# The end of a fused attention and mixture-of-experts kernel: two instead of four dense steps held back, and the second expert layer and the output by halves of the columns

## The chip, the cores and the metric

The kernel runs on one core of one Trainium2 chip. The metric is the device time of one execution in microseconds (us); the figure for a kernel is the median of its runs.

## What is computed

Three stages follow each other: an attention with a learned relative bias, a dense two-layer network on its result, and a soft mixture of eight experts. The end of the kernel, where the change lies, is the last of them:

```python
logits = x @ phi                          # x: 2304 x 512 (the dense stage's result), phi: 512 x 32
d = softmax over the tokens of logits     # 2304 x 32
slot_input = (d.T @ x).reshape(8, 4, 512) # eight experts, four slots each
for e in range(8):
    h = np.maximum(slot_input[e] @ w1[e], 0.0)   # w1: 8 x 512 x 1024
    slot_out[e] = h @ w2[e]                      # w2: 8 x 1024 x 512
c = softmax over the slots of logits      # 2304 x 32
out = c @ slot_out.reshape(32, 512)       # 2304 x 512
```

## The kernel before

The dense stage (class `Moe`) takes the 2304 tokens in six blocks of 384 and the hidden width in 16 steps of 128, 96 steps in all. A step has an up-projection (`up`, line 686: 12 matmuls of 384 columns into `h`), a leaky activation on ScalarE and VectorE that ends in a high part and a low part of `g` (lines 694 to 706), and a down-projection (`down`, line 718: three groups of three matmuls of 512 columns, one group for each 128 tokens, into `ys`). The weights of a step are split into a high and a low part, held in one of four pairs of buffers, `h0`/`l0` to `h3`/`l3` (`wpairs`). A pair is written again four steps later. In the trace they are `w76h`, `w76l` and so on; 76 to 79 are the last four steps.

The down-projections of the last `LATE_DOWN` steps are held back until after the loop (line 966). They are then issued, in an order written out by hand in `LATE_ORDER` (lines 55 to 60), between the pieces of the routing of the last block. There ("D", i, t) is the group t of the i-th held-back step and stays in program order on TensorE. "E" copies a finished `ys` out of PSUM, "T" turns it, "L" computes the logits, "N" and "K" the softmax over the tokens, "B" turns logits and weights back, "G" sums up the slot inputs, "M" merges. The result, `rows`, is turned once more (line 1065) and copied into `sst`, the stationary operand of the first expert layer.

The expert stage (class `Experts`) reads 64 tiles of expert weights, each 128 x 1024 in fp32 (512 KB): 32 of `w1` and 32 of `w2`, in the order of `self.order` (line 1021). `load` (line 1023) puts the next tile of that order into the buffer it is handed, called a home. There are 37 homes: five in `pre` (loaded two blocks ahead), three in `ex`, 15 in `ep` (the dense stage's raw weight buffers, freed step by step), five in `er` (a ring over memory that the dense stage gives back), one in `g32` and eight in `em`, the four weight pairs. Those of `er`, `g32` and `em` are asked for when the dense stage is over, in `Experts.run` (lines 1044 to 1048). The other 27 tiles go into homes that the first expert layer has finished with (line 1088). All DMAs of this stretch are issued by SyncE, in one queue. A scheduler that models the timeline when the program is built puts each engine's instructions in order; that order is fixed on the chip.

A tile belongs to expert 4k + j, and its matmuls write the 32 rows 32j to 32j + 31 of PSUM, so that four tiles with different j can use four column groups of TensorE beside each other. The first layer writes `hps` (two banks of 512 columns), the second `ops` (one bank of 512 columns). An fp32 matmul call shows as two instructions in the trace, so a tile is four instructions in either layer. Between the layers `hps` goes through the ReLU and is turned into `gst` (line 1096). After the second layer `ops` is copied and corrected into `st` (lines 1106 and 1107), multiplied by the token weights `cT` for 18 groups of 128 tokens (line 1114), copied out of PSUM by ScalarE and VectorE in turn (lines 1116 and 1118), and written by nine DMAs of 512 KB (line 1119) from homes that are free.

Of the kernel before, what the change touches and what calls it, by code (L numbers as in the profile page):

```python
# [8 lines left out]
F32 = mybir.dt.float32  # L9
F32R = mybir.dt.float32r  # L10
# [3 lines left out]
AF = mybir.ActivationFunctionType  # L14
ALU = mybir.AluOpType
AX = mybir.AxisListType
PSUM = bass.MemoryType.PSUM
DRAM = bass.MemoryType.DRAM

P = 128  # L20
B, H, S, D = 4, 8, 576, 64
HP = H // 2
N = B * S
DM = H * D
DFF = 2048
NF = DFF // P
NC = DM // P
SLOTS = 32
E = 8
SPE = SLOTS // E  # L30
F2 = 1024
NT = 384
NBLK = N // NT
# [15 lines left out]
ERING = 5  # L49
# [1 line left out]
XF = 10  # L51
LAG = 2
WL_DVE = ((0, 3), (0, 4), (0, 5), (0, 6), (0, 7), (0, 8), (0, 11), (0, 13), (0, 14), (1, 2), (1, 3), (1, 4), (1, 5), (1, 6), (1, 9), (1, 10), (1, 12), (1, 13), (2, 0), (2, 1), (2, 3), (2, 9), (2, 12), (2, 13), (2, 15), (3, 4), (3, 9), (3, 11), (3, 13), (3, 15), (4, 5), (4, 8), (4, 9), (4, 12), (4, 13), (4, 14), (5, 3), (5, 4), (5, 5), (5, 7), (5, 8), (5, 9), (5, 12))
LATE_DOWN = 4
LATE_ORDER = (
# [4 lines left out]
)  # L60
GL_POOL = (0,)
# [481 lines left out]
class Moe:  # L543
# [134 lines left out]
    def up(self, n):  # L678
        nc = self.nc
        blk, f = self.seq[n]  # L680
        xh, xl = self.x[blk]
        wh, wl = self.ws[blk if blk > 1 else 0, f]
        h = self.ps_h.tile([P, NT], F32, tag="h", name=f"h{n}")
        for c in range(NC):
            for n_, (w_, x_) in enumerate(((wh, xh), (wh, xl), (wl, xh))):
                nc.tensor.matmul(  # L686
                    h,
                    w_[:, c * P : (c + 1) * P],
                    x_[:, c],
                    start=c == 0 and n_ == 0,  # L690
                    stop=c == NC - 1 and n_ == 2,
                )
        g = self.g32[:, NT * (n % 2) : NT * (n % 2) + NT]
        nc.scalar.activation(g, h, AF.Relu)  # L694
        neg = self.g32[:, 2 * NT : 3 * NT]
        nc.scalar.activation(neg, h, AF.Relu, scale=-1.0)  # L696
        nc.vector.scalar_tensor_tensor(g, neg, self.nal[:, f : f + 1], g, ALU.mult, ALU.add)  # L697
        hold = n == NBLK * NF - LATE_DOWN
        if hold:
            gh, gl = (p.tile([P, NT], F32R, tag=tag, name=f"{tag}_{n}") for p, tag in self.raws)  # L700
        else:
            gh, gl = (self.gr[:, NT * k : NT * k + NT] for k in (self.ng % 3, 3 + self.ng % 3))
            self.ng += 1
        nc.scalar.activation(gh, g, AF.Copy)  # L704
        eng = nc.gpsimd if blk in GL_POOL else nc.vector
        eng.tensor_tensor(gl, g, gh.bitcast(F32), ALU.subtract)  # L706
        return gh, gl
# [301 lines left out]
class Experts:  # L1009
# [3 lines left out]
    def __init__(self, nc, w1, w2):  # L1013
        self.nc = nc
        self.tiles = []
        self.homes = []
        self.free = []
        w1 = w1.rearrange("e (p c) n -> e p c n", c=NC)
        w2 = w2.rearrange("e (p a b) n -> e p a (b n)", a=4, b=2)

        self.order = [(w, k, a, j) for w in (w1, w2) for k in range(2) for a in range(4) for j in range(4)]

    def load(self, home):

# [10 lines left out]
    def run(self, tc, moe, scon, out, more):  # L1035
        nc = self.nc
        cT, sst = moe.cT, self.sst.rearrange("p (e c m) -> p e c m", e=E, c=NC)
        with ExitStack() as ctx:
            er = ctx.enter_context(tc.tile_pool(name="e_ring", bufs=1, reuse_waits="tile"))
            ep = ctx.enter_context(tc.tile_pool(name="e_sb", bufs=1, reuse_waits="tile"))  # L1040
            ps_a = ctx.enter_context(tc.tile_pool(name="e_ps_a", bufs=1, space=PSUM, reuse_waits="tile"))
            ps_b = ctx.enter_context(tc.tile_pool(name="e_ps_b", bufs=5, space=PSUM, reuse_waits="tile"))

            for n in range(ERING):
                self.load(lambda k, n=n: er.tile([P, 1024], F32, tag=f"er{n}", name=f"er{k}"))
            self.load(lambda k: moe.g32[:, :1024])
            for pool, tag in more:
                self.load(lambda k, pool=pool, tag=tag: pool.tile([P, 1024], F32, tag=tag, name=f"em{k}"))
            sc = ep.tile([P, P + 1], F32, name="sc")
            nc.sync.dma_start(sc, scon)  # L1050
            gst = ep.tile([P, E, 8, SLOTS], F32, name="gst")
# [19 lines left out]
                do["S"](ep, "cs", ps_b)  # L1071

            hps = ps_a.tile([P, 2, 512], F32, name="hps")
            ops = ps_a.tile([P, 512], F32, name="ops")
            hs = ep.tile([P, 1024], F32, name="hs")
            for n, (w, k, a, j) in enumerate(self.order):
                t = self.tiles[n]
                rows = slice(32 * j, 32 * j + 32)
                first, last = k == 0 and a == 0, k == 1 and a == 3
                for b in range(2):  # L1080
                    if n < 32:
                        dst, lhs = hps[rows, b], sst[:, 4 * k + j, a]
                        f, l = first, last
                    else:
                        dst, lhs = ops[rows], gst[:, 4 * k + j, 2 * a + b]
                        f, l = first and b == 0, last and b == 1
                    nc.tensor.matmul(dst, lhs, t[:, 512 * b : 512 * b + 512], start=f, stop=l)  # L1087
                self.load(self.homes[n])
                if n == 31:
                    nc.scalar.activation(hs[:, :512], hps[:, 0], AF.Relu)  # L1090
                    nc.vector.tensor_scalar(hs[:, 512:], hps[:, 1], 0.0, None, ALU.max)
                    for h in range(2):
                        tp = ps_b.tile([P, 4, P], F32, tag="b", name=f"turn1_{h}")
                        for c in range(4):
                            lhs = hs.rearrange("r (p c) -> r c p", c=8)[:, 4 * h + c]
                            nc.tensor.matmul(tp[:, c], lhs, sc[:, :P], start=True, stop=True)  # L1096
                        for g in range(2):
                            src = tp.rearrange("p c (j k m) -> p k j c m", k=2, m=16)[:, g]
                            fill(g, gst[:, 4 * g : 4 * g + 4, 4 * h : 4 * h + 4, 16 * g : 16 * g + 16], src)


            hi = ep.tile([P, 512], F32R, name="hi")
            st = ep.tile([P, 512], F32R, name="st")
            for h in range(2):
                c = slice(256 * h, 256 * h + 256)
                nc.scalar.activation(hi[:, c], ops[:, c], AF.Copy)
                nc.vector.scalar_tensor_tensor(
                    st[:, c], hi[:, c].bitcast(F32), sc[:, P:], ops[:, c], ALU.mult, ALU.add
                )
            for t in range(0, N // P, 2):  # L1110
                os_ = self.free.pop(0)(f"o{t}").rearrange("p (a n) -> p a n", a=2)
                for a in range(2):
                    o = ps_b.tile([P, 512], F32, tag="b", name=f"o{t}_{a}")
                    nc.tensor.matmul(o, cT[:, (t + a) * P : (t + a + 1) * P], st, start=True, stop=True)
                    if a:
                        nc.vector.tensor_copy(os_[:, a], o)
                    else:
                        nc.scalar.activation(os_[:, a], o, AF.Copy)
                nc.sync.dma_start(out[t * P : (t + 2) * P].rearrange("(a p) n -> p a n", p=P), os_)


@with_exitstack
def kernel(
    ctx, tc, qk, v_l, cpack, w_l, alpha, phi, mw1, mw2, lcol, prow, xmain, xtail, scon, out
):
    nc = tc.nc
# [67 lines left out]
    def prefetch(n):  # L1194
        f = n - (NBLK - 1) * NF
        if n == 4 * NF:
            t = set0["bias"].tile([P, 9 * S], F32, tag="nb", name="pre")
            for j in range(5):
                ex.load(lambda k, j=j: t[:, 1024 * j : 1024 * j + 1024])
        elif f == XF:  # L1200
            t = x0.tile([P, 3072], F32, tag="x", name="ex")
            for j in range(3):
                ex.load(lambda k, j=j: t[:, 1024 * j : 1024 * j + 1024])

        if f == -2:
            ex.sst = moe.raw_tile(0, "sst")
            nc.gpsimd.memset(ex.sst, 0.0)
        if 1 <= f + 3 < NF:
            ex.load(lambda k: moe.raw_tile(f + 3, f"ep{k}"))

    with ExitStack() as mctx:
        moe.run(mctx, phi, prefetch)
    more = [(kp, t) for t in ("h0", "l0", "h1", "l1")] + [(ws, t) for t in ("h2", "l2", "h3", "l3")]
    ex.run(tc, moe, scon, out, more)


# [31 lines left out]
def _layout(i):  # L1248
# [29 lines left out]
        alpha=i["moe_alpha"].reshape(NF, P).T,  # L1278
        phi=i["moe2_phi"].reshape(NC, P, 2, 4, SPE).transpose(1, 0, 3, 2, 4).reshape(P, NC, SLOTS),
        mw1=i["moe2_w1"],  # L1280
        mw2=i["moe2_w2"],
    )


# [27 lines left out]
```

## Time and profile before

| | us |
|---|---|
| median of 3 runs | 828.95 |
| lowest and highest | 828.21 and 831.59 |
| the profiled execution | 829.09 |
| span of the profiled execution, first to last instruction | 827.3 |

The profile is of one execution. Its engines are PE (TensorE matmul), PEld (TensorE weight load, which overlaps PE), DVE (VectorE), ACT (ScalarE), POOL (GpSimd) and SP (SyncE; SPq is its queue). Times in a row are us from the start of the span unless marked ns, and L1087 is line 1087 of the kernel before. `out<-in` names what an instruction writes and reads, x32 is a count, and what stands in brackets is the idle time before the first of the row and what ended it. PEclk is the granted TensorE clock as a share of full speed.

### The profile page before, as it was taken

The numbers are of one execution on the slowest core, as the hardware profiler recorded it, in microseconds if no ns is written. First come the engines' busy times: TensorE is split into PE (matmuls) and PEld (weight loads), VectorE is DVE, ScalarE is ACT, GpSimd is POOL, SyncE is SP. The second block draws the span as 40 slices with busy tenths as digits, with TensorE's granted clock in tenths as the row PEclk, the third lists the DMA queues.
The fourth block names the chain that finished last, engine by engine and source line by source line (L and its number), as shares of the span: only waits on it lengthen the run. The fifth ranks groups of instructions, "written<-read, shape, count | busy, mean of one in ns | idle before, by whom it ended". The sixth has DMA issues, their size and how long they took to land.

```text
span 827.3 us, 18364 instructions
## 1 busy us (share of the span) xinstructions
PE 769.7 (93%) x7428; PEld 639.3 (77%) x7428; DVE 552.8 (67%) x951; ACT 487.3 (59%) x961; POOL 339.6 (41%) x259
## 2 busy tenths in 40 slices
PE   6876699999999999999999999999999999998993
PEld 6766577778777768988888988888889898885431
DVE  8956668888898857776778565655675756565003
ACT  8852477888888874444356566656566656554002
POOL 6974324546467532113224454445444551231000
PEclk9989789999999999999999999999999999999998
DMA  6799894956844351342240011301100134338996
GB/s 211 184 220 204 196 251 147 235 168 187 239 137 146 95 176 70 114 153 101 103 128 1 1 29 42 134 1 39 39 1 21 29 114 141 90 115 298 383 363 229
DMA packets 59493, 114.44 MB, mean 138 GB/s; under 512 B 10640, under 2 KB 38160, under 8 KB 57360
## 3 DMA queue, kind: packets, MB, share of 16 engines
q1 hardware_dynamic: 59408, 113.26, 45.2%
q8 instruction: 58, 0.95, 0.5%
q14 instruction: 27, 0.22, 0.1%
HBM read 91.95 MB, written 21.29 MB: 137 GB/s over the span
## 4 chain that ended last, share of the span: by engine, by line
PE 82%; DVE 7%; issue 4%; ACT 2%; DMA 2%; POOL 2%; DVEq 0%; ACTq 0%; SPq 0%; POOLq 0%
PE h L686 23%; PE ys L718 22%; PE o L467 10%; PE s L381 8%; PE acc L161 5%; PE t L439 5%; PE ops L1087 3%; PE hps L1087 2%; DVE mask L145 1%; DVE z L399 1%; PE lp L778 1%; DMA W<-rows 1%; DVE r L485 1%; PE turn L1096 0%; DVE x L605 0%
## 5 line engine op out<-in xcount | busy, mean ns | idle before, releaser
L697 DVE SCALAR_TENSOR_TENSOR g<-g,nal 128x384 f32<-128x384 f32 x96 | 99.6, 1038 | 83.1 <-ACT g L696 82.9
L419 ACT ACTIVATE e<-z,m 128x576 f32<-128x576 f32 x144 | 109.9, 767 | 17.6 <-DVE m L399 17.6
L399 DVE CUSTOM_DVE_ANT_0 z<-s,nb 128x576 f32<-128x576 f32 x144 | 108.1, 755 | 17.3 <-PE s L381 10.5
L704 ACT ACTIVATE gr<-g 128x384 fp32r<-128x384 f32 x95 | 49.7, 523 | 85.7 <-DVE g L697 85.6
L467 PE MATMUL o<-g,v 128*64 128x256 f32 (+1 forms) x640 | 87.4, 419 | 0.5 <-ACT g L455 0.5
L455 ACT ACTIVATE g<-t 128x640 f32<-128x640 f32 x96 | 67.2, 703 | 34.6 <-PE t L439 30.8
L694 ACT ACTIVATE g<-h 128x384 f32<-128x384 f32 x96 | 46.8, 488 | 57.4 <-PE h L686 55.1
L161 PE MATMUL acc<-wp,mask 128*128 128x64 bf16 (+1 forms) x1680 | 58.6, 200 | 21.2 <-issue 11.9
L706 DVE TENSOR_TENSOR gr<-g,gr 128x384 fp32r<-128x384 f32 x79 | 53.5, 677 | 34.0 <-ACT gr L704 31.7
L161 PEld LDWEIGHTS <-mask 128*128 128x128 bf16 (+1 forms) x1680 | 56.6, 105 | 23.1 <-issue 14.3
L439 PE MATMUL t<-ident,e 64*128 64x64 f32 x1440 | 68.8, 224 | 5.0 <-DVE m L399 3.0
L439 PEld LDWEIGHTS t<-ident,e 64*128 64x128 f32 x1440 | 66.0, 140 | 7.3 <-issue 5.0
L381 PE MATMUL s<-kh,qh 64*128 64x288 f32 x320 | 61.9, 382 | 8.0 <-DVE rows L186 5.2
L467 PEld LDWEIGHTS o<-g,v 128*64 128x64 f32 x640 | 44.1, 139 | 29.4 <-issue 1.5
L142 ACT ACTIVATE mask<-pr,wb 128x576 bf16<-128x576 f16 (+4 forms) x81 | 47.0, 665 | 22.4 <-PE acc L161 22.4
L354 POOL TENSOR_SCALAR qh<-raw 128x1216 fp32r<-128x1216 f32 x16 | 19.4, 1214 | 79.7 <-PE s L381 75.6
L706 POOL TENSOR_TENSOR gr<-g,gr 128x384 fp32r<-128x384 f32 x16 | 19.6, 1228 | 78.4 <-ACT gr L704 68.6
L381 PE MATMUL s<-kl,qh 64*128 64x288 f32 x320 | 48.6, 299 | 0.0
L381 PE MATMUL s<-kh,ql 64*128 64x288 f32 x320 | 48.5, 298 | 0.0
L696 ACT ACTIVATE g<-h 128x384 f32<-128x384 f32 x96 | 46.6, 485 | 0.0
L381 PEld LDWEIGHTS s<-kh,qh 64*128 64x128 f32 x320 | 31.8, 194 | 17.5 <-issue 7.2
L356 POOL TENSOR_TENSOR ql<-raw,qh 128x1216 fp32r<-128x1216 f32 x16 | 44.7, 2795 | 0.0
(986 smaller groups left out, 2045.4 us busy)
## 6 DMA issues: line engine op xcount, KB each, us to landing
wide<-in_w_dram SPq DMA_DIRECT2D x16, 1024.0 KB
ep<-in_mw_dram SPq DMA_DIRECT2D x30, 512.0 KB
raw<-in_qk_dram SPq DMA_DIRECT2D x16, 896.0 KB
nb<-W SPq DMA_DIRECT2D x12, 576.0 KB
v<-in_v_l_dram SPq DMA_DIRECT2D x16, 320.0 KB
pre<-in_mw_dram SPq DMA_DIRECT2D x10, 512.0 KB
er<-in_mw_dram SPq DMA_DIRECT2D x9, 512.0 KB
em<-in_mw_dram SPq DMA_DIRECT2D x8, 512.0 KB
```

The source lines that it names most:

```text
L161: nc.tensor.matmul(dst[:, u // 8, :, :, 4 * (u % 8) : 4 * (u % 8) + 4], mask[:, (16 * k + u) % RING, cols], wp[:, part], start=part == 0, ...
L381: nc.tensor.matmul(s[:, hf, :288], st["q", a][d, o : o + P], st["k", b][d, 288 * h : 288 * h + 288], start=n_ == 0, stop=n_ == len(seq) - 1,),
L399: self.nc.vector.tensor_tensor_reduce(out=z.rearrange("p (a b) -> p a b", a=2), in0=s[:, :, :288], in1=self.nb[st["hp"]][:, slot].rearrang ...
L419: self.nc.scalar.activation(e, z, AF.Exp, bias=m, scale=-1.0, accum_out=st["sum"][:, slot : slot + 1]),
L439: self.pin(i, nc.tensor.transpose(tp[:, r, 64 * c : 64 * c + 64], e[q, k0 : k0 + P], self.ident[q, q]))
L455: self.pin(i, nc.scalar.activation(dst, src, AF.Copy))
L467: nc.tensor.matmul(op[64 * h : 64 * h + 64, 0, :n], st["v"][:, h, c], g[:, h, c], start=c == 0, stop=c == 4),
L686: nc.tensor.matmul(h, w_[:, c * P : (c + 1) * P], x_[:, c], start=c == 0 and n_ == 0, stop=c == NC - 1 and n_ == 2,)
L697: nc.vector.scalar_tensor_tensor(g, neg, self.nal[:, f : f + 1], g, ALU.mult, ALU.add)
L704: nc.scalar.activation(gh, g, AF.Copy)
L706: eng.tensor_tensor(gl, g, gh.bitcast(F32), ALU.subtract)
L718: i = self.nc.tensor.matmul(self.ys[blk][t], g_[:, t * P : (t + 1) * P], w_[:, 512:], start=f == 0 and n_ == 0, stop=f == NF - 1 and n_ == 2,)
```

## The change

Two down-projections instead of four are held back: those of steps 76 and 77 run in the loop, and `LATE_ORDER` is shorter by their six groups. The separate buffers of the first held-back step's `g` are gone. The weight pairs of these two steps are asked for in `prefetch`, right behind their down-projections; the two other pairs, `g32` and then the ring follow after the loop, so the same 37 homes are taken in another order. `w2` is laid out on the host by halves of its columns: 16 tiles carry columns 0 to 255, 16 tiles columns 256 to 511, and a tile holds four blocks of 256 columns in place of two of 512. The second layer runs the first 16 tiles, then `finish(0)`, then the other 16, then `finish(1)`. `finish` copies and corrects that half, multiplies it by the token weights, and writes it with five DMAs (four of 512 KB, one of 256 KB), whose rows in memory are 256 columns long. `ops` takes two banks of PSUM, and the pool of the turns and outputs four instead of five.

```diff
...
 XF = 10
 LAG = 2
-LATE_DOWN = 4
+LATE_DOWN = 2
 LATE_ORDER = (
-    ("D", 0, 0), ("D", 1, 0), ("D", 2, 0), ("D", 0, 1), ("D", 1, 1), ("D", 3, 0), ("E", 0), ("D", 2, 1),
-    ("D", 3, 1), ("E", 1), ("D", 0, 2), ("T", 0), ("D", 1, 2), ("T", 1), ("D", 2, 2),
-    ("D", 3, 2), ("E", 2), ("L", 0), ("L", 1), ("N", 0), ("K", 0), ("T", 2), ("L", 2), ("N", 1),
+    ("D", 0, 0), ("D", 1, 0), ("E", 0), ("D", 0, 1), ("D", 1, 1), ("E", 1), ("T", 0), ("D", 0, 2), ("T", 1), ("D", 1, 2),
+    ("E", 2), ("L", 0), ("L", 1), ("N", 0), ("K", 0), ("T", 2), ("L", 2), ("N", 1),
     ("B", 0), ("K", 1), ("B", 1), ("G", 0), ("G", 1), ("M",),
 )
 GL_POOL = (0,)
...
         neg = self.g32[:, 2 * NT : 3 * NT]
         nc.scalar.activation(neg, h, AF.Relu, scale=-1.0)
         nc.vector.scalar_tensor_tensor(g, neg, self.nal[:, f : f + 1], g, ALU.mult, ALU.add)
-        hold = n == NBLK * NF - LATE_DOWN
-        if hold:
-            gh, gl = (p.tile([P, NT], F32R, tag=tag, name=f"{tag}_{n}") for p, tag in self.raws)
-        else:
-            gh, gl = (self.gr[:, NT * k : NT * k + NT] for k in (self.ng % 3, 3 + self.ng % 3))
-            self.ng += 1
+        gh, gl = (self.gr[:, NT * k : NT * k + NT] for k in (self.ng % 3, 3 + self.ng % 3))
+        self.ng += 1
         nc.scalar.activation(gh, g, AF.Copy)
         eng = nc.gpsimd if blk in GL_POOL else nc.vector
         eng.tensor_tensor(gl, g, gh.bitcast(F32), ALU.subtract)
...
         self.homes = []
         self.free = []
         w1 = w1.rearrange("e (p c) n -> e p c n", c=NC)
-        w2 = w2.rearrange("e (p a b) n -> e p a (b n)", a=4, b=2)
-
-        self.order = [(w, k, a, j) for w in (w1, w2) for k in range(2) for a in range(4) for j in range(4)]
+        self.order = [(w1, k, a, j) for k in range(2) for a in range(4) for j in range(4)]
+        self.order += [(w2[c], k, a, j) for c in range(2) for k in range(2) for a in range(2) for j in range(4)]
 
     def load(self, home):
 
...
             er = ctx.enter_context(tc.tile_pool(name="e_ring", bufs=1, reuse_waits="tile"))
             ep = ctx.enter_context(tc.tile_pool(name="e_sb", bufs=1, reuse_waits="tile"))
             ps_a = ctx.enter_context(tc.tile_pool(name="e_ps_a", bufs=1, space=PSUM, reuse_waits="tile"))
-            ps_b = ctx.enter_context(tc.tile_pool(name="e_ps_b", bufs=5, space=PSUM, reuse_waits="tile"))
-
-            for n in range(ERING):
-                self.load(lambda k, n=n: er.tile([P, 1024], F32, tag=f"er{n}", name=f"er{k}"))
+            ps_b = ctx.enter_context(tc.tile_pool(name="e_ps_b", bufs=4, space=PSUM, reuse_waits="tile"))
+
             self.load(lambda k: moe.g32[:, :1024])
             for pool, tag in more:
                 self.load(lambda k, pool=pool, tag=tag: pool.tile([P, 1024], F32, tag=tag, name=f"em{k}"))
+            for n in range(ERING):
+                self.load(lambda k, n=n: er.tile([P, 1024], F32, tag=f"er{n}", name=f"er{k}"))
             sc = ep.tile([P, P + 1], F32, name="sc")
             nc.sync.dma_start(sc, scon)
             gst = ep.tile([P, E, 8, SLOTS], F32, name="gst")
...
                 do["S"](ep, "cs", ps_b)
 
             hps = ps_a.tile([P, 2, 512], F32, name="hps")
-            ops = ps_a.tile([P, 512], F32, name="ops")
+            ops = ps_a.tile([P, 2, 512], F32, name="ops")
             hs = ep.tile([P, 1024], F32, name="hs")
+            hi = ep.tile([P, 2, 256], F32R, name="hi")
+            st = ep.tile([P, 2, 256], F32R, name="st")
+
+            def finish(c):
+
+                nc.scalar.activation(hi[:, c], ops[:, c, :256], AF.Copy)
+                nc.vector.scalar_tensor_tensor(
+                    st[:, c], hi[:, c].bitcast(F32), sc[:, P:], ops[:, c, :256], ALU.mult, ALU.add
+                )
+                for t in range(0, N // P, 4):
+                    m = min(4, N // P - t)
+                    os_ = self.free.pop(0)(f"o{t}_{c}")[:, : 256 * m].rearrange("p (a n) -> p a n", a=m)
+                    for a in range(0, m, 2):
+                        o = ps_b.tile([P, 2, 256], F32, tag="b", name=f"o{t}_{a}_{c}")
+                        for k in range(2):
+                            q = (t + a + k) * P
+                            nc.tensor.matmul(o[:, k], cT[:, q : q + P], st[:, c], start=True, stop=True)
+                        if a:
+                            nc.vector.tensor_copy(os_[:, a : a + 2], o)
+                        else:
+                            nc.scalar.activation(os_[:, a : a + 2], o, AF.Copy)
+                    nc.sync.dma_start(
+                        out[t * P : (t + m) * P, 256 * c : 256 * c + 256].rearrange("(a p) n -> p a n", p=P), os_
+                    )
+
             for n, (w, k, a, j) in enumerate(self.order):
                 t = self.tiles[n]
                 rows = slice(32 * j, 32 * j + 32)
-                first, last = k == 0 and a == 0, k == 1 and a == 3
-                for b in range(2):
-                    if n < 32:
-                        dst, lhs = hps[rows, b], sst[:, 4 * k + j, a]
-                        f, l = first, last
-                    else:
-                        dst, lhs = ops[rows], gst[:, 4 * k + j, 2 * a + b]
-                        f, l = first and b == 0, last and b == 1
-                    nc.tensor.matmul(dst, lhs, t[:, 512 * b : 512 * b + 512], start=f, stop=l)
+                if n < 32:
+                    first, last = k == 0 and a == 0, k == 1 and a == 3
+                    for b in range(2):
+                        nc.tensor.matmul(
+                            hps[rows, b], sst[:, 4 * k + j, a], t[:, 512 * b : 512 * b + 512], start=first, stop=last
+                        )
+                else:
+                    c = (n - 32) // 16
+                    for b in range(4):
+                        nc.tensor.matmul(
+                            ops[rows, c, :256],
+                            gst[:, 4 * k + j, 4 * a + b],
+                            t[:, 256 * b : 256 * b + 256],
+                            start=k + a + b == 0,
+                            stop=(k, a, b) == (1, 1, 3),
+                        )
                 self.load(self.homes[n])
                 if n == 31:
                     nc.scalar.activation(hs[:, :512], hps[:, 0], AF.Relu)
...
                         for g in range(2):
                             src = tp.rearrange("p c (j k m) -> p k j c m", k=2, m=16)[:, g]
                             fill(g, gst[:, 4 * g : 4 * g + 4, 4 * h : 4 * h + 4, 16 * g : 16 * g + 16], src)
-
-
-            hi = ep.tile([P, 512], F32R, name="hi")
-            st = ep.tile([P, 512], F32R, name="st")
-            for h in range(2):
-                c = slice(256 * h, 256 * h + 256)
-                nc.scalar.activation(hi[:, c], ops[:, c], AF.Copy)
-                nc.vector.scalar_tensor_tensor(
-                    st[:, c], hi[:, c].bitcast(F32), sc[:, P:], ops[:, c], ALU.mult, ALU.add
-                )
-            for t in range(0, N // P, 2):
-                os_ = self.free.pop(0)(f"o{t}").rearrange("p (a n) -> p a n", a=2)
-                for a in range(2):
-                    o = ps_b.tile([P, 512], F32, tag="b", name=f"o{t}_{a}")
-                    nc.tensor.matmul(o, cT[:, (t + a) * P : (t + a + 1) * P], st, start=True, stop=True)
-                    if a:
-                        nc.vector.tensor_copy(os_[:, a], o)
-                    else:
-                        nc.scalar.activation(os_[:, a], o, AF.Copy)
-                nc.sync.dma_start(out[t * P : (t + 2) * P].rearrange("(a p) n -> p a n", p=P), os_)
+                if n in (47, 63):
+                    finish((n - 47) // 16)
 
 
 @with_exitstack
...
             nc.gpsimd.memset(ex.sst, 0.0)
         if 1 <= f + 3 < NF:
             ex.load(lambda k: moe.raw_tile(f + 3, f"ep{k}"))
+        if 0 <= f - (NF - 4) < 4 - LATE_DOWN:
+            pool, *tags = moe.wpairs[f - (NF - 4)]
+            for tag in tags:
+                ex.load(lambda k, tag=tag: pool.tile([P, 1024], F32, tag=tag, name=f"em{k}"))
 
     with ExitStack() as mctx:
         moe.run(mctx, phi, prefetch)
-    more = [(kp, t) for t in ("h0", "l0", "h1", "l1")] + [(ws, t) for t in ("h2", "l2", "h3", "l3")]
+    more = [(pool, t) for pool, *tags in moe.wpairs[4 - LATE_DOWN :] for t in tags]
     ex.run(tc, moe, scon, out, more)
 
 
...
         alpha=i["moe_alpha"].reshape(NF, P).T,
         phi=i["moe2_phi"].reshape(NC, P, 2, 4, SPE).transpose(1, 0, 3, 2, 4).reshape(P, NC, SLOTS),
         mw1=i["moe2_w1"],
-        mw2=i["moe2_w2"],
+        mw2=i["moe2_w2"].reshape(E, P, 2, 4, 2, 256).transpose(4, 0, 1, 2, 3, 5).reshape(2, E, P, 2, 1024),
     )
 
 
```

## Rows read from the trace of the kernel before

**Rows 1.** The chain of waits in order of time: start us, us, what.

```profile
742.34 6.26 PE ys L718 x27
...
763.31 5.93 PE hps L1087 x32
...
786.05 22.54 PE ops L1087 x128
```

**Rows 2.** Windows: start:end length, busy us of each engine, PEclk, DMA share, GB/s.

```profile
744.00:745.00 1.00, 1.00 (x6) 0.81 (x6) 0.61 (x1) 0.36 (x1) 0.00 (x0) 1.00 0.00 0
768.00:770.00 2.00, 2.00 (x19) 0.51 (x15) 0.32 (x2) 0.35 (x1) 0.00 (x0) 1.00 0.95 278
804.00:805.00 1.00, 1.00 (x4) 0.25 (x3) 0.00 (x0) 0.00 (x0) 0.00 (x0) 1.00 0.31 123
813.00:814.00 1.00, 1.00 (x5) 0.43 (x4) 1.00 (x3) 1.00 (x3) 0.00 (x0) 1.00 0.99 371
825.00:826.00 1.00, 0.00 (x0) 0.00 (x0) 0.00 (x0) 0.00 (x0) 0.00 (x0) 0.50 0.51 186
```

**Rows 3.** DMA packets from 776 to 803 us, while weights arrive.

```profile
DMA packets 3038, 11.08 MB, mean 410 GB/s; under 512 B 339, under 2 KB 339, under 8 KB 3036
```

**Rows 4.** DMA packets from 814 to 824 us, while the output leaves.

```profile
DMA packets 1954, 3.78 MB, mean 378 GB/s; under 512 B 112, under 2 KB 112, under 8 KB 1953
```

**Rows 5.** SyncE's queue in order of time: start us, us, what is issued.

```profile
745.79 0.33 SPq L1031 DMA_DIRECT2D g<-in_mw_dram  x1
748.40 4.92 SPq L1031 DMA_DIRECT2D em<-in_mw_dram  x8
...
766.96 2.62 SPq L1031 DMA_DIRECT2D pre<-in_mw_dram  x5
...
792.69 4.15 SPq L1031 DMA_DIRECT2D er<-in_mw_dram  x4
```

**Rows 6.** Order of time, TensorE's weight loads in the second layer, early and late.

```profile
793.30 0.20 PEld L1087 LDWEIGHTS ops<-ep,gst 128*32 128x32 f32 x4 [0.23 <-issue]
793.73 0.20 PEld L1087 LDWEIGHTS ops<-ep,gst 128*32 128x32 f32 x4 [0.23 <-issue]
...
804.18 0.14 PEld L1087 LDWEIGHTS ops<-er,gst 128*32 128x32 f32 x2 [0.29 <-DMA er<-in_mw_dram]
804.64 0.11 PEld L1087 LDWEIGHTS ops<-er,gst 128*32 128x32 f32 x1 [0.32 <-issue]
805.07 0.11 PEld L1087 LDWEIGHTS ops<-er,gst 128*32 128x32 f32 x1 [0.32 <-issue]
805.42 0.14 PEld L1087 LDWEIGHTS ops<-er,gst 128*32 128x32 f32 x2 [0.24 <-DMA er<-in_mw_dram]
```

**Rows 7.** Order of time around dense step 79: weight load, last up-projection matmul, low half.

```profile
740.31 0.19 PEld L686 LDWEIGHTS h<-x,w79l 128*128 128x128 f32 x1 [0.66 <-POOL w79l L675]
...
742.00 0.34 PE L686 MATMUL h<-x,w79l 128*128 128x384 f32 x1
...
745.20 0.56 DVE L706 TENSOR_TENSOR gr<-g,gr 128x384 fp32r<-128x384 f32 x1 [0.59 <-ACT gr L704]
```

**Rows 8.** Line 1114, the output matmuls' weight loads: ns min/median/max, first and last start.

```profile
L1114 PEld LDWEIGHTS o<-st,cT x18: 186/187/190, 810.6 to 815.2; 128*128 128x128 f32 x18
```

**Rows 9.** Order of time, TensorE, two transposes between waves of `hps`.

```profile
768.63 0.61 PE L1087 MATMUL hps<-ep,sst 128*32 128x512 f32 x3
769.17 0.44 PE L887 MATMUL tc<-ident,cs 128*128 128x128 f32 x2
769.54 3.68 PE L1087 MATMUL hps<-ep,sst 128*32 128x512 f32 x32
```

**Rows 10.** Order of time after the second layer: the copy and `st`.

```profile
808.61 0.38 ACT L1106 ACTIVATE hi<-ops 128x256 fp32r<-128x256 f32 x1 [22.14 <-PE ops L1087]
809.03 0.48 DVE L1107 SCALAR_TENSOR_TENSOR st<-hi,sc,ops 128x256 fp32r<-128x256 f32 x1 [22.10 <-ACT hi L1106]
```

**Rows 11.** DMA packets from 40 to 60 us, a stretch of small packets.

```profile
DMA packets 6310, 4.78 MB, mean 239 GB/s; under 512 B 1660, under 2 KB 6264, under 8 KB 6306
```

## The prediction, made before the changed kernel was built or run

> **What bounds the kernel now.** I read the chain that ended last in order of time, then the stretches from 738 us on in short windows, then the queue of SyncE, then TensorE's own order. The change touches nothing before 734 us. From there the chain [rows 1] is TensorE nearly without a break: dense matmuls to about 752, a routing tail through ACT and DVE, the first expert layer from 763.3, the turn of its result, and the second expert layer, 22.5 us of `ops` from 786.05 to 808.6. Then comes a tail with little on TensorE. The windows [rows 2] show the other resource. The DMA engines are idle at 744 to 745, then busy with weights until about 804.5, and busy again, with the output, from 813.0 to 825.5. Weights move at 410 GB/s in 4 KB packets [rows 3], the output at 378 GB/s in 2 KB packets [rows 4].
>
> The queue [rows 5] shows who feeds whom. SyncE issues the load into `g32` at 745.8, eight into the weight pairs from 748.4, the ring's behind them, and the first refill only at 767.0, after the first wave of `hps` has freed a buffer. The last four weights go out from 792.7.
>
> TensorE's order explains the 22.5 us. Four tiles of one round fill four column groups. Early in the layer weight loads come in fours every 0.43 us [rows 6]: four instructions per wave, a tile (four instructions) costs 0.43 us. Late, they come as two, one, one within 1.24 to 1.28 us: each tile runs by itself, since its four instructions add to the same rows of PSUM one behind the other. Of the 32 tiles the last 10 or so (from 795.2) go like that: 22 x 0.43 + 10 x 1.3 = 22.5, the row. Data ended at 804.5, TensorE at 808.6: the end of this layer is TensorE's, with the weights close behind.
>
> **Part 1: two steps held back, not four.** No work goes away. Down 76 and 77 (27 matmuls took 6.26 us [rows 1], so 0.232 each, nine per step = 2.09 us) now run in the loop, ahead of the up-projection of 79. Before, that up-projection waited 0.7 us for POOL's `w79l` [rows 7]; with the downs ahead of it that wait goes. In exchange a wait appears. The low half of 79's `g` came 3.4 us after its `h` (742.34 to 745.76 [rows 7]). Five thirds of down steps (0.70 each) covered that; now one does, D(0,0), and D(1,0) needs `g` of 79. The wait is at most 3.4 - 0.7 = 2.7 us; ScalarE is freer than it was, which takes off some 0.7, so 2.0. Queued behind it on TensorE are all pinned D steps, and behind those the turns, logits and sums. The rest of the tail (E, T, L, N, B, G) has the same instructions with less cover. Working it through by the durations above, the last D ends about 1.0 us later, and so does `hps`: 764.3. Bounds: 0 (the waits cancel) to 2.7.
>
> **Part 2: buffers taken sooner.** Four loads (2.1 MB, 5.1 us at 410 GB/s) move from 748 to about 740 to 745, where the queue was nearly empty. SyncE waits there in order for down 76, then 77; behind it stand only `g32` and the other expert loads, and none is needed before 763. I cost this at nothing, gain included. There are 37 buffers as before, and the other 27 tiles can't go out before `hps` frees one. Before, the backlog ended just as the refills began (768 to 770 is the dip, 278 GB/s [rows 2]); now it ends earlier and the engines idle until the first refill at about 768. The 27 refills end 1.0 us later than before: 805.5.
>
> **Part 3: second layer by halves.** 64 calls of 512 columns become 128 of 256: the same columns. First half: 32 waves of 0.215 = 7.0 us if waves of four keep up. The four weight loads of a wave span 0.20 us [rows 6], so it is close; at 0.25 it is 8.0. I take 7.0: 787.0 to 794.0. All its 16 tiles are there by then (tile 47 is the eleventh refill, about 784). A tile that runs alone now has a chain of eight instructions of 0.213, one overlapped with the next tile: 1.5 us, where it was 1.28.
>
> Then 18 output matmuls of 256 columns join TensorE's queue before or among the second half. Their weight loads take 187 ns each [rows 8], more than the 0.117 us that 256 columns would stream at the rate of the `ys` matmuls [rows 1]: 18 x 0.18 = 3.2 us. The far bounds are 2.1 us (streaming alone) and 4.4, which is nine interruptions at the price of the two transposes that broke into `hps`: start to start 0.91 instead of 0.42 [rows 9], 0.49 each. I take 3.2, as it rests on the same instruction.
>
> That price has a rule beside it: the Trainium skill, TensorEngine Tiling (Array Packing), Key Properties, says that changing the tiling mode drains the engine, and this change puts full-width matmuls among column-tiled ones. By that rule alone the 4.4 would hold and the forecast would rise by 1.2 us.
>
> Second half: 16 x 0.43 = 6.9 us, plus 1.07 us (1.5 - 0.43) for each tile that runs alone. How many? Before, TensorE met the arrivals with 10 tiles left at 795.2. Now it stands there at 787.0 + 7.0 + 3.2 + 6 x 0.43 = 799.8, 4.6 us later, while arrivals shift by 1.0. Of the 3.6 us in hand each tile eats 0.86 (arrivals every 1.29, four-wide 0.43): 4.2 tiles, so 5.8 are left. The layer ends at 787.0 + 7.0 + 3.2 + 6.9 + 5.8 x 1.07 = 810.3, against 808.6. Bounds: 808.4 (no tile short of the data; last landing plus one chain of eight, with no shift from part 1) and 814.8 (10 alone, as before).
>
> **Part 4: output by halves.** Before, from the layer's end: copy and `st` twice [rows 10], data moving at 813.0 (4.4 us), 12.5 us of transfer, 1.8 us to the end of the span: 18.7. Now one half's copy and `st` (0.38 + 0.48 and two gaps of 0.04) come before the first output matmul, so data move 3.6 us after the end, and half as many bytes follow. The first half's output (2.36 MB) is queued when the last weights have been issued (about 798) and moves behind them from 805.5. Its rows are now 1 KB. Per engine, 4 KB packets take 160 ns (410 / 16) and 2 KB packets 86.7 ns (378 / 16); a line through both gives 50 ns for 1 KB, which is 328 GB/s, 7.2 us per half (an estimate from [rows 3, 4]). Bounds: 6.2 us at the 2 KB rate, 9.9 at the 239 GB/s of a stretch whose packets average 757 B [rows 11]. I stay at 7.2, nearest to the output's own row.
>
> The Trainium skill, DMA: Bandwidth & Descriptors, Why small descriptors are slow, gives a fixed cost of about 3 cycles per packet beside one per 32 bytes; an estimate by that is 35 beats for 32 of data, 0.957 of the 2 KB rate, 6.5 us per half and a forecast 0.7 us lower.
>
> The first half is out by 805.5 + 7.2 = 812.7, before the second starts at 810.3 + 3.6 = 813.9, so the covered half is free. Evacuation (nine copies of 0.6 to 0.7 us on two engines) stays under the transfer.
>
> **Sum.** Span after: 810.3 + 3.6 + 7.2 + 1.8 = 822.9, against 827.3. The profiled execution took 829.09 us for that span, 1.8 more, and 0.14 over the median of 828.95. So 822.9 + 1.8 = 824.7 us. Put otherwise: about 7 us come off the tail, 1.0 goes back in the held-back steps and 0.7 more in the second layer, and 1.0 to the smaller rows is inside the 7.
>
> **Rivals.** (a) The gain in full: no shift from part 1, TensorE close to the data, output rows as fast as 2 KB ones: 808.4 + 3.6 + 6.2 + 1.8 = 820.0, so 822 us. For it: the weights did end 4 us ahead of TensorE. Against: the wait for `g` of 79 is plain. (b) As many tiles run alone as before: 814.8, span 827.4, 829.2 us, no change. For it: the order is fixed when the program is built, and that they ran alone though the data were there late in the layer shows that it does not follow the chip. (c) The first half's output gets into SyncE's queue ahead of the last weights, 7.2 us later for these, landing 812.7, layer end 816.6, 831.0 us. Against: the last weights are issued by 797.8, the first output is ready at about 796.6, so at most a few cross. (d) Slower: all 16 tiles of the second half run alone, at 1.5 us: 787.0 + 7.0 + 3.2 + 24 = 821.2, span 833.8, 835.6 us. It turns into a loss from 10 tiles alone. For it: chains are now eight long; against: most of these tiles have landed by 798. That the earlier loads themselves bring something would show as an earlier last landing; I count it in (a).
>
> **How the numbers follow.** Forecast 50%, its own range 822.5 to 827; (a) 16%, (b) 17%, (c) 6%, (d) 11%. Half a per cent (4.1 us, about what a measurement tells from no change) sets the limits at 824.8 and 833.1. The forecast lies on the first, so its chance splits, 28 to 22. Faster: 28 + 16 = 44%. Same: 22 + 17 + 5 = 44%. Slower: 11 + 1 = 12%. The range, 821 to 831, leaves out (d) and the ends of (a) and (c).
>
> **What would show it.** A wait of about 2 us of an `ys` matmul for `gr` near 746; `hps` starting near 764.3; DMA idle before 768; the last weights landing near 805.5; `ops` of the first half in some 7 us; five or six tiles at 1.5 us; output moving without a gap behind the weights, and 7 us of it after the layer's end. The prediction is wrong if `hps` starts earlier than 763, if the weight loads of the second half come singly from its first tile, or if 1 KB rows move below 280 GB/s.

## The result and the profile after

| | before | after |
|---|---|---|
| median, us | 829.84 (5 runs, 828.21 to 831.59) | 839.35 (5 runs, 834.34 to 839.75) |
| the profiled execution, us | 829.09 | 837.57 |
| its span, us | 827.3 | 835.8 |

The ratio is 1.0108, interval [1.0077, 1.0138]: slower by 1.1%, where 824.7 us and at most 831 were forecast.

The profile stays the place to see where. Stretches far ahead of the change differ by some microseconds between profiled executions (the first matmul of step 75's up-projection stands between 719.1 and 724.0 us in the eleven profiles of this study), so I count from that instruction: 723.10 before, 722.67 after.

| from, to | before, us | after, us | difference |
|---|---|---|---|
| up 75 to first `hps` | 40.21 | 41.92 | +1.71 |
| first `hps` to second layer | 22.74 | 22.63 | -0.11 |
| second layer, to its last end | 22.54 | 36.75 | +14.21 |
| its end to the end of the span | 18.71 | 11.83 | -6.88 |
| sum | 104.20 | 113.13 | +8.93 |

The chain of waits of the changed kernel in order of time (start us, us, what; it answers to [rows 1]):

```profile
747.66 2.47 PE ys L713 x9
...
764.59 5.69 PE hps L1101 x32
...
787.22 16.24 PE ops L1107 x128
803.48 0.39 ACT hi L1075
803.90 0.49 DVE st L1076
804.44 1.21 PE o L1086 x8
805.65 4.09 PE ops L1107 x30
809.74 1.15 PE o L1086 x8
810.89 2.74 PE ops L1107 x18
813.63 0.43 PE o L1086 x2
814.07 9.90 PE ops L1107 x80
...
824.94 2.91 PE o L1086 x18
```

The first half of the second layer took 16.24 us, where 7.0 was forecast. The second took 20.5: 16.7 in `ops`, 2.8 in the 18 output matmuls, and 1.0 in which TensorE stood still for the first half's `hi` and `st`.

TensorE's order of time shows how its tiles pass. Each row is a run of matmuls that read the same kind of buffer; the start is what matters here, since four instructions of one tile follow each other in steps of 0.21 us:

```profile
792.60 0.40 PE L1107 MATMUL ops<-pre,gst 128*32 128x256 f32 x1
792.81 0.38 PE L1107 MATMUL ops<-er,gst 128*32 128x256 f32 x1
792.84 0.38 PE L1107 MATMUL ops<-pre,gst 128*32 128x256 f32 x1
793.02 0.38 PE L1107 MATMUL ops<-er,gst 128*32 128x256 f32 x1
793.05 0.38 PE L1107 MATMUL ops<-pre,gst 128*32 128x256 f32 x1
793.24 0.38 PE L1107 MATMUL ops<-er,gst 128*32 128x256 f32 x1
793.27 4.17 PE L1107 MATMUL ops<-pre,gst 128*32 128x256 f32 x34
797.07 0.40 PE L1107 MATMUL ops<-ep,gst 128*32 128x256 f32 x1
...
814.00 3.05 PE L1107 MATMUL ops<-ex,gst 128*32 128x256 f32 x21
816.67 0.40 PE L1107 MATMUL ops<-ep,gst 128*32 128x256 f32 x1
```

The first `pre` tile enters beside the last four instructions of an `er` tile: two tiles run beside each other, never four. The next kind of buffer follows after five tiles (797.07 - 792.60) and after three (816.67 - 814.00): 0.89 us a tile, 4.2 steps of 0.2135. Before, a tile passed in 0.43 [rows 6]. None of these rows has a wait in brackets. The windows (start:end length, busy us of PE, PEld, DVE, ACT, POOL, then PEclk, DMA share, GB/s) show the other resource:

```profile
766.00:768.00 2.00, 2.00 (x12) 0.39 (x5) 0.39 (x3) 0.00 (x0) 0.00 (x0) 0.50 0.22 80
...
786.00:788.00 2.00, 2.00 (x7) 1.28 (x7) 0.47 (x2) 0.38 (x1) 0.00 (x0) 0.50 1.01 395
788.00:790.00 2.00, 2.00 (x13) 0.97 (x13) 0.10 (x1) 0.00 (x0) 0.00 (x0) 0.69 1.03 416
...
818.00:824.00 6.00, 5.95 (x50) 3.23 (x46) 0.00 (x0) 0.01 (x1) 0.00 (x0) 1.00 0.00 0
```

For the last 6 us of the layer nothing moves at all: all weights are there, the first half's output is gone. The queue of SyncE answers to [rows 5]:

```profile
768.24 2.40 SPq L1025 DMA_DIRECT2D pre<-in_mw_dram  x5
...
793.57 4.16 SPq L1025 DMA_DIRECT2D em<-in_mw_dram  x4
805.96 0.40 SPq L1091 DMA_DIRECT2D out_dram<-g  x1
...
826.49 4.74 SPq L1091 DMA_DIRECT2D out_dram<-ero  x5
```

The refills follow `hps` as they did, and the first half's output is issued at 806.0, not at about 798 as forecast.

### The profile page after: what moved, and what is told of

Same layout as the page of the kernel before. It is cut to its first block, busy times and chain, and to the rows that moved or that the text cites. A ratio compares the mean times of both kernels' runs of the same rounds, so it can differ in the third digit from the quotient of the medians.

```text
span 835.8 us, 18663 instructions
## 1 busy us (share of the span) xinstructions
PE 779.1 (93%) x7574; PEld 651.0 (78%) x7574; DVE 550.0 (66%) x950; ACT 488.0 (58%) x962; POOL 339.0 (41%) x259
## 4 chain that ended last, share of the span: by engine, by line
PE 83%; DVE 6%; issue 4%; DMA 2%; ACT 2%; POOL 1%; SPq 0%; DVEq 0%; ACTq 0%; POOLq 0%
PE h L685 23%; PE ys L713 21%; PE o L466 10%; PE s L380 8%; PE t L438 5%; PE acc L160 5%; PE ops L1107 4%; PE hps L1101 2%; DMA W<-rows 2%; DVE mask L144 1%; PE lp L773 1%; DVE z L398 1%; PE o L1086 1%; PE turn L1122 1%; DVE r L484 1%
```

## The experiments

**The theory** after this result: what costs the time is the length of a run, the number of instructions that a column group gets behind one another. Program order is tile by tile in both kernels: the programs as built hand TensorE the calls of this layer so, the scheduler did not mix the tiles, and what runs beside what is therefore settled on the chip. As long as a tile is four instructions, TensorE lets the next groups pass beside it; with eight, about four of them stand in the way until they have gone through. **The rivals**: the output matmuls among the tiles, the two steps that are no longer held back, narrower instructions that cost more in themselves, and the reading of the prediction, that tiles run alone where TensorE's order puts them so. Time ratios are to runs of the kernel before on the same chip; "stretch" is the time from up 75 to the end of the span, 104.20 before and 113.13 after.

**The changed kernel with the second layer in turns**, one call of each of the four tiles, then the next:

```diff
-                else:
+                elif j == 3:
...
-                    for b in range(4):
...
+                    for b0 in range(0, 4, 1):
+                        for i in range(4):
+                            for b in range(b0, b0 + 1):
+                                nc.tensor.matmul(
+                                    ops[32 * i : 32 * i + 32, c, :256],
...
```

> The changed kernel with one edit: in the second expert layer the four tiles of a round take turns call by call (block of columns outside, tile inside), so a column group gets two instructions at a visit instead of eight. Theory 1 (runs): TensorE takes its instructions in order and holds only about four for one column group, so eight behind each other for one group keep the other groups waiting; turns bring back waves of four at 0.215 us, 7 to 8 us per half instead of 16.2, the first half's output then fills the time of the last weights, layer end near 809, 821 to 824 us. Theory 2 (price of the instruction): a 256-column matmul with its weight load costs about 0.12 us whatever the order; then 836 to 839 us, as the changed kernel.

821.65 us, ratio 0.9931 [0.9909, 0.9953], stretch 98.92. Its chain, and a piece of TensorE's order:

```profile
785.99 8.07 PE ops L1109 x128
...
806.71 1.93 PE ops L1109 x26
808.66 0.39 ACT hi L1075
```

```profile
789.08 0.38 PE L1109 MATMUL ops<-er,gst 128*32 128x256 f32 x1
789.09 0.39 PE L1109 MATMUL ops<-pre,gst 128*32 128x256 f32 x3
789.30 0.38 PE L1109 MATMUL ops<-er,gst 128*32 128x256 f32 x1
789.30 0.39 PE L1109 MATMUL ops<-pre,gst 128*32 128x256 f32 x3
...
806.71 1.91 PE L1109 MATMUL ops<-em,gst 128*32 128x256 f32 x26 [0.63 <-DMA em<-in_mw_dram]
```

Four tiles start together every 0.21 us, the first half takes 8.07 us (PEclk is 0.51 from 786 to 788), and the layer ends on the landing of the last weights: the last tile waits for it until 806.71. The same matmuls, with as many output matmuls among them, take 14.2 us less in the stretch: the order alone makes the loss, and the narrow instructions in themselves do not.

**Two calls at a visit**, so runs of four instructions (the edit is against the kernel with turns):

```diff
-                    for b0 in range(0, 4, 1):
+                    for b0 in range(0, 4, 2):
...
-                            for b in range(b0, b0 + 1):
+                            for b in range(b0, b0 + 2):
```

> As the kernel with turns, but two calls (four instructions) at a visit. Theory 1 with four held for a column group: the same time as with turns call by call, within 1 us. Theory 1 with fewer than four held: a tile of four instructions still blocks, 827 to 832 us. Theory 2: 836 to 839 us.

822.32 us, 0.9945 [0.9919, 0.9971], stretch 98.67: as with one. Runs of four still pass beside each other.

**Three calls, then one** (runs of six and two; the edit is against the kernel with two calls):

```diff
-                    for b0 in range(0, 4, 2):
+                    for b0 in (0, 3):
...
-                            for b in range(b0, b0 + 2):
+                            for b in range(b0, min(b0 + 3, 4)):
```

> The changed kernel with the second layer's round visited in turns of three calls and then one, so that a column group gets six instructions behind one another and later two. If a tile of eight costs 0.895 us because about four instructions of a run can be held back while the next group's go on, the next group starts with the third of the six, and the rounds of the first half come at about 10 to 12 slots of 0.2135 us, where turns of one or two calls need 8 and whole tiles 16.8: the first half takes about 9 to 11 us (it took 8.07 with turns of one call, 16.24 as changed), and the whole stays at 822 to 825 us, since the last tiles wait for their landing. If any run that is longer than four goes two wide as a run of eight does, the first half takes about 13 us or more.

One execution; its chain:

```profile
789.37 10.08 PE ops L1109 x128
```

The first half took 10.08 us, inside the 9 to 11 of the theory and not the 13 of a sharp limit. PEclk was 1.00 there, so the times to set beside it are those at full clock further down: 7.11 us in turns and 15.26 us with runs of eight. The whole was 828.4 us, 3 above the range given: by then TensorE and not the landing ended the second half (6.88 us for its last 84 instructions).

**The kernel before with runs of eight in its first layer** (two tiles of one column group behind each other, 512 columns as ever):

```diff
+                    if a % 2 and j == 3:
+                        for i in range(4):
+                            for a_ in (a - 1, a):
...
+                                for b in range(2):
```

> The kernel before, the first expert layer alone reordered: two tiles of one column group behind each other, so eight instructions of 512 columns per visit instead of four; same matmuls, same sums. If about four are held for a group: the next group starts with the fifth of the eight, 16 visits of 4 x 0.427 = 1.71 us and a tail of 1.7, plus about 3 for the half clock at its start: hps takes 29 to 32 us instead of 17.2. If the changed kernel's slowness was that of 256 columns: hps stays 17 to 18 us.

One execution, 836.96 us. The chain:

```profile
759.35 11.70 PE hps L1086 x32
...
771.41 8.79 PE hps L1086 x32
...
780.47 15.79 PE hps L1086 x64
...
801.84 14.41 PE ops L1097 x128
```

The layer took 37 us, where it took 17.3 (763.31 [rows 1] to 780.6, the start of the ReLU), with neither the halves nor the output near it, and none of its matmul rows behind the first has a wait in brackets. That is more than was expected, in its first round above all, which ran partly at half clock (PEclk 0.50 from 759 to 765). The other two parts give the same period as the changed kernel: eight steps of 0.427 for the last run, and (15.79 - 3.42) / 7 = 1.77 us for each before it, 4.1 steps. And the second layer, untouched, then took 14.41 us, since its weights had long landed.

**Two steps held back, alone, in the kernel before** (the early loads and the order of homes with it):

```diff
-LATE_DOWN = 4
+LATE_DOWN = 2
...
+        if 0 <= f - (NF - 4) < 4 - LATE_DOWN:
+            pool, *tags = moe.wpairs[f - (NF - 4)]
```

> The kernel before with the first two parts of the change alone: two steps held back, their pairs loaded sooner, order of the homes as changed; second layer and output as before. If the wait for the activation of step 79 is the price and the earlier loads bring nothing: 1.0 to 1.5 us slower than before, 830.5 to 831.5. If the earlier loads pay: as before or up to 4 us faster, 825 to 830.

828.75 us, 1.0014 [0.9998, 1.0029], stretch 106.31, 2.1 more: by the time it can't be told from no change, and the earlier loads do not pay. TensorE's order shows the wait, and a window of 2 us shows DMA engines that have run out of homes:

```profile
744.08 0.51 PE L713 MATMUL ys<-w79h,gr 128*128 128x512 f32 x1 [1.54 <-ACT gr L699]
```

```profile
763.00:765.00 2.00, 2.00 (x16) 0.51 (x12) 0.00 (x0) 0.00 (x0) 0.00 (x0) 0.68 0.00 1
```

**The changed kernel with four held back**, tile by tile as it was:

```diff
-LATE_DOWN = 2
+LATE_DOWN = 4
```

> The changed kernel with four steps held back again (order by hand, separate buffers and pairs as before); halves of the columns stay. If holding back two costs what the trace shows (hps 1.3 us later), and the earlier loads bring nothing: 1.0 to 1.5 us faster than the changed kernel, 836 to 838. If the earlier loads are worth their 5 us of transfer: slower than the changed kernel, 841 to 844.

```profile
787.23 15.26 PE ops L1112 x128
```

833.25 us, 1.008 [1.0049, 1.0111], stretch 110.80: still slower. The stretch is 2.3 of the 8.9 shorter: 1.7 in `hps`, which starts 40.17 us after up 75 again, and 1.0 in the first half of `ops`, less 0.4 between the layers. Only the 1.7 can be put down to holding back. The 1.0 is the clock: this half ran at a PEclk of 1.00, while the changed kernel had 0.50 from 786 to 788 and 0.69 from 788 to 790, by which some 2.0 us of its 16.24 ran at half speed. With two held back the clock can be 1.00 there as well: it was so with three calls and then one, and with the other order of the held-back steps below.

**Four held back and turns of one call**, both edits at once:

> The turns of e1_round together with four steps held back (as e3_hold4). If the two costs are separate (two held back costs 1.2 us by e4_hold2_only, 6 us were the gap of e3 to the changed kernel across two calls): 1 us faster than e1_round, ratio to before 0.990 to 0.993. If the last weights or the output set the end whatever the start of the first layer: as e1_round, 0.993.

```profile
787.26 2.13 PE L1114 MATMUL ops<-er,gst 128*32 128x256 f32 x33
...
792.26 2.11 PE L1114 MATMUL ops<-ep,gst 128*32 128x256 f32 x34
```

820.25 us, 0.9912 [0.988, 0.9944], stretch 97.27: the shortest median of all, ahead of both kernels. Against turns with two held back it is 1.65 us shorter in the stretch; the intervals of the two ratios overlap. The first half of `ops` took 7.11 us (787.26 to 794.37) with a PEclk of 1.00.

**The kernel before with its second layer in turns**:

```diff
+                    for b in range(2):
+                        for i in range(4):
...
+                                ops[32 * i : 32 * i + 32],
```

> The kernel before, the second layer alone in turns (one call of each of the four tiles of a round in turn). The prediction read the last ten tiles at 1.28 us each as chains that TensorE's own order makes. If so, turns shorten the layer from 22.5 to 18 to 19 us and the kernel by 3 to 4 us. If these tiles came at the pace of their landing (512 KB at 410 GB/s is 1.28 us too): no change, within 0.2%.

827.06 us, 1.0015 [0.9988, 1.0042]: no change. TensorE's order near the end:

```profile
800.50 1.04 PE L1089 MATMUL ops<-er,gst 128*32 128x512 f32 x2 [0.23 <-DMA er<-in_mw_dram]
801.74 1.04 PE L1089 MATMUL ops<-er,gst 128*32 128x512 f32 x2 [0.20 <-DMA er<-in_mw_dram]
802.98 1.90 PE L1089 MATMUL ops<-er,gst 128*32 128x512 f32 x10 [0.19 <-DMA er<-in_mw_dram]
```

Each tile waits for its landing, 1.24 us after the one before. So the last ten tiles of the kernel before ran alone because they arrived alone. In its own trace the first weight load of eight of these ten has a DMA in brackets, down to the very last tile:

```profile
806.67 0.14 PEld L1087 LDWEIGHTS ops<-er,gst 128*32 128x32 f32 x2 [0.26 <-DMA er<-in_mw_dram]
```

**Turns, and a different order of the held-back steps**, all of step 78's groups ahead of those of 79:

```diff
-    ("D", 0, 0), ("D", 1, 0), ("E", 0), ("D", 0, 1), ("D", 1, 1), ("E", 1), ("T", 0), ("D", 0, 2), ("T", 1), ("D", 1, 2),
+    ("D", 0, 0), ("D", 0, 1), ("D", 0, 2), ("D", 1, 0), ("E", 0), ("D", 1, 1), ("E", 1), ("T", 0), ("D", 1, 2), ("T", 1),
```

> As e1_round, with another order by hand of the two held-back steps: all three groups of the first step, then those of the second. The wait for the activation of step 79 (1.54 us in the changed kernel) should shrink to 0.2 or less, with less cover later for the copies and turns. If the wait is the price of holding back two: 0.5 to 1.3 us faster than e1_round. If the later cover is worth as much: the same.

```profile
745.86 0.50 PE L713 MATMUL ys<-w79h,gr 128*128 128x512 f32 x1 [0.17 <-ACT gr L699]
```

The wait for `g` of 79 fell from 1.54 to 0.17 us, and nothing came of it: 822.13 us, 0.9938 [0.9914, 0.9961], and `hps` starts 42.29 us after up 75 (41.89 in the same kernel without the edit). The routing behind the downs waits later by as much: `sp` now starts behind `dT` of VectorE at 758.8.

## Why the prediction was wrong, step by step

**Part 1 held in kind and was short in size.** The wait of an `ys` matmul for `gr` is 1.54 us (2.0 taken, at most 2.7); `hps` starts 1.71 us later against up 75, where 1.0 was taken. The bounds of 0 to 2.7 hold it. Taking the wait away (0.17 us in the last experiment) did not bring `hps` forward, so the thinner cover behind it, which the prediction named too, is worth as much as the wait; the two were not told apart further.

**Part 2 held.** The early loads bring nothing: the DMA engines idle until the first refill at 768.2 (a share of 0.22 in 766 to 768, the 0.00 above with that part alone). But the end of the weights was read too early. I took the fall of the DMA share at 804.5 [rows 2] for the end of the data. In the kernel before the windows behind it still show

```profile
805.00:806.00 1.00, 1.00 (x5) 0.36 (x4) 0.00 (x0) 0.00 (x0) 0.00 (x0) 1.00 0.13 53
806.00:807.00 1.00, 1.00 (x6) 0.25 (x3) 0.00 (x0) 0.00 (x0) 0.00 (x0) 1.00 0.01 4
```

and a tile is there when its last packet is: the last one of the kernel before was waited for until 806.67. Few of the 16 engines at work are not "done". The low bound of 808.4 in part 3 does not follow from the 804.5 (a chain of eight behind it, 1.7 us, ends at 806.2); it is what 806.7 gives.

**Part 3 failed, twice.** First, its reading of [rows 6]. The late tiles were called alone by TensorE's own order. The rows that I quoted say otherwise: the first weight load of a tile, at 804.18 and at 805.42, has its releaser in brackets, the DMA of its buffer. A 512 KB tile takes 1.28 us at 410 GB/s [rows 3], which is the interval (1.24 between those two). So the kernel before was bound by arrivals there; that its order does not matter is shown by its second layer in turns, at no change. Rival (b) rested on the same misreading. Second, the step "32 waves of 0.215 = 7.0 us if waves of four keep up". I priced the "if" by the weight loads' 0.20 us, and never asked how TensorE comes to interleave tiles that the program gives it one behind the other. It does so by letting the next group's instructions go past the present group's, and it does that for a run of four (and for two), less for six, and two wide for eight. At full clock the first half takes 7.11 us in turns, 10.08 with runs of six and 15.26 with runs of eight (16.24 as changed, 2.0 us of it at half clock). I had even written that a chain was now eight long, and used it only for tiles that run alone.

The rest of part 3 was of the right size: the 18 output matmuls take 2.8 us (3.2 taken, 2.1 to 4.4 as bounds). The Trainium skill, TensorEngine Tiling (Array Packing), Key Properties, names a drain at a change of tiling mode, by which the 4.4 would have held. The trace does not show it at that price.

**Part 4 held.** From the layer's end to the end of the span it is 11.8 us (12.6 taken). The 1 KB rows move faster than the 328 GB/s taken; packets from 829 to 833 us:

```profile
DMA packets 1373, 1.37 MB, mean 343 GB/s; under 512 B 40, under 2 KB 1372, under 8 KB 1372
```

An estimate by the Trainium skill, DMA: Bandwidth & Descriptors, Why small descriptors are slow, is 0.957 of the 378 GB/s of [rows 4], 362: the measurement, 343, lies between that and the 328.

**The rivals.** (d), all tiles of the second half alone, 835.6 us, had the right sign and nearly the time, but not the mechanism: the tiles pass in pairs, in both halves, and the first half alone lost 9.2 us that (d) left at 7.0. What I gave it against, "most of these tiles have landed by 798", was true and beside the point. The kernel that the sum described is the one in turns: stretch 98.92, 5.3 less than before, where the sum had 4.4 less. Its layer ends 87.06 us after up 75 (808.64), where the sum had 87.2, but that closeness is in part luck: it ends there by a last landing at 806.71 with 26 matmuls behind it, not by five or six tiles that run alone.

**Left open.** Why about four instructions of a run stand in the way was not taken apart: runs of two, four, six and eight fit it, but no run here shows the queue itself, and since every call here is two instructions, four instructions can't be told from two calls. Nor was the clock at the second layer's start settled: 0.50 in 786 to 788 as changed and 0.51 in turns, but 1.00 in both kernels with four held back and in two of those with two (three calls then one, the other order of the held-back steps), about 1 us (16.24 against 15.26).

## What to carry to other kernels

Where column groups of TensorE are to run beside each other, count the instructions that one group gets in a row in the program, and keep it at four or fewer by turning among the groups (two and four ran four wide here, six and eight did not; five was not run). Making calls narrower without that doubles the run and can cost more than the stage gained. When rows show work one by one, read the releaser of each piece's first instruction before blaming the order, and compare the interval with bytes over bandwidth. An end of data is the last packet, not the fall of the mean share.

## What was not expected of the hardware

The same 128 matmuls of 256 columns took 7.11, 10.08 and 15.26 us at full clock for runs of two, six and eight instructions in a column group, with no wait in the rows shown of the first half, and runs of eight made a first layer of 512 columns 37 us long instead of 17.3. Rows of 1 KB left at 343 GB/s, 0.91 of the 378 of 2 KB rows.
